# Attention and two expert layers in one program: another rate for recording attention, and another start for the second head pair

## The chip, the cores and the metric

The kernel runs on one core of a Trainium2 chip. The metric is the device time of one execution in microseconds (us), the median of several. A core has TensorE (PE, matrix products; its weight loads are PEld in the profile), VectorE (DVE), ScalarE (ACT), GpSimd (POOL) and SyncE (SP, which here issues DMAs). Each runs its own instructions in their order and waits on semaphores for the others.

## What is computed

Attention over 4 batches and 12 heads, 448 tokens of 64 features, with normalized queries and keys; then two expert layers over all 1792 tokens, the first with an ELU, the second gated, with a norm before it.

```python
def rmsnorm(x, g):
    rms = np.sqrt(np.mean(x * x, axis=-1, keepdims=True) + 1e-06)
    return x / rms * g
q_n, k_n = (rmsnorm(q, g_q), rmsnorm(k, g_k))
scores = np.matmul(q_n, k_n.transpose(0, 1, 3, 2)) / np.sqrt(64)
attn = softmax(scores)
x = np.matmul(attn, v)              # heads side by side: 1792 x 768

h = x @ w_in                        # 768 -> 2048
x = np.where(h > 0, h, np.exp(np.minimum(h, 0)) - 1) @ w_out

xn = rmsnorm(x, rms_g)
g = xn @ w_gate                     # 768 -> 1536
x = (g / (1 + np.exp(-g)) * (xn @ w_val)) @ w_out2
```

## The kernel before

**Tiles and stages.** Attention goes by head pairs: six pairs to a batch (NPB), 24 in all, numbered 0 to 23. All products of the experts split both operands into a rounded high part and the rest and run three matmuls of 128 x 448 each (`mm3`). The experts run in five stages (STAGES): first experts of batch 0, first experts of batch 1, second experts of both, first experts of batches 2 and 3, second experts of both. A first-expert stage has 16 units of six products with `xs` (the split x) and 24 units of four with `gbig` (the split activations). x of batch b is complete when its six pairs are; tile `xf` is a pair's result.

**A pair.** `load_tk` loads token rows, `squares` sums their squares (ACT, then DVE at line 555), `factors` makes the reciprocal roots `rr` of one or more pairs with 13 small DVE instructions (`rsqrt`), and `spread` spreads the factors of a pair's keys over the partitions: for pairs under FIRST by eight small matmuls against `ident` into a PSUM bank, for the others by a write to DRAM (`scr`) and two loads back (`rb`). `prep_q` and `prep_k` split queries and keys; `prep_k` multiplies by the spread factors (line 355, `rw` or, for odd pairs of batch 0, a part of `wr`). Then four groups of scores (`s_group`): matmuls, maxima (line 636, tile `nm`), a multiplication of the maxima by `rr` (line 638), exponentials (ACT, tile `p` or `pj`; for odd pairs of batch 0 a part of `tbig`). The tail of a pair is eight rounds of transposes (line 308) and copies into `pt` and `pe` and three to four products with the values. A pair counts 15 pieces: 4 groups of scores, 8 transposes, 3 products.

**Weights.** A weight chunk of 128 x 768 arrives as 64-bit floats (`wr<-wst`) and is converted once by four instructions into `wc` (two on ACT or POOL, two on DVE: lines 506 and 355), then split: a copy `w<-wc` (ACT or POOL) and a subtraction `w<-wc,w` (POOL or DVE, line 338 or 340). The 32 chunks of the first experts are kept in DRAM for the later stages.

**What sets the order.** The program is first recorded as a list of operations; `Plan.schedule` then gives each an engine and a place. It goes by estimated costs, engine by engine; of the operations that are ready it takes the one recorded first, and an operation that may run on several engines goes where it is estimated to end first. So the place in the recording is a priority. Recording: `phase(0)` records the six pairs of batch 0 (90 pieces); then each stage records its units one by one and between them pieces of the next pairs, at an even rate that reaches GOALS[s] pairs by the end of the stage: 12, 19, 24, 24, 24. Stage 1 needs pairs 6 to 11, stage 3 needs all 24. `norm` (square root on ACT with its own table, reciprocal on DVE) is recorded behind a first-expert stage.

**PSUM.** In `phase(0)` four banks take scores, three transposes, one the values' products and the spread factors; from `phase(1)` on it is two, two, one, and three for the experts' products.

## Time and profile before

| | us |
|---|---|
| median of 3 runs | 1361.91 |
| lowest and highest | 1359.98, 1365.45 |
| the profiled execution | 1362.41 |
| its span, first to last instruction | 1360.6 |
| PE busy in it | 1295.2 |
| DVE, ACT, POOL busy | 683.4, 642.0, 748.2 |

The mean granted clock of TensorE is 0.983 of full speed; the slices of the page with less than the full clock all lie in the first 374 us. A matmul's busy time is modelled and overlaps its neighbours, so a busy PE is not one at its peak: what a stretch yields is better told by how many matmuls it holds. The first expert matmul starts at 113.8 us, the second stage's first at 316.8, the third's at 525.6; the last pair's result is there at 827.2 us.

### The profile page before, as it was taken

How to read it: one execution, taken by the hardware profiler on the slowest of the kernel's cores; microseconds unless marked ns; L12 is line 12 of the kernel's file. 1: busy time of each engine (PE TensorE's matmuls, PEld its weight loads, DVE VectorE, ACT ScalarE, POOL GpSimd, SP SyncE). 2: the span in 40 equal slices, each digit the busy share in tenths (PEclk: the TensorE clock that was granted, in tenths of full speed). 3: DMA queues.
4: the chain of work that ended last, by engine and by line, in shares of the span. 5: the costliest groups of instructions: out<-in, count | busy, mean ns of one | idle time of the engine just before them, and what ended most of it. 6: DMA issues, size and time to landing. Idle time of an engine off the chain costs nothing.

```text
span 1360.6 us, 17489 instructions
## 1 busy us (share of the span) xinstructions
PE 1295.2 (95%) x6438; PEld 1058.2 (78%) x6438; DVE 683.4 (50%) x997; ACT 642.0 (47%) x1251; POOL 748.2 (55%) x571
## 2 busy tenths in 40 slices
PE   4788989988899999999999999999999999999998
PEld 2345766666577777788888788999999989999998
DVE  5686899886444559953656553102221552132332
ACT  5674767576655666655553452433223532221220
POOL 1354976684564668644564466536345664354450
PEclk9798999989999999999999999999999999999999
DMA  5466777782343445654453425221111211111112
GB/s 182 154 207 216 257 242 237 244 276 82 103 124 109 135 136 167 234 168 145 154 162 121 151 98 175 79 59 47 58 59 47 59 47 58 55 51 59 47 35 81
DMA packets 63142, 174.15 MB, mean 128 GB/s; under 512 B 11200, under 2 KB 20688, under 8 KB 63056
## 3 DMA queue, kind: packets, MB, share of 16 engines
q1 hardware_dynamic: 54064, 163.58, 37.0%
q10 hardware_dynamic: 8992, 9.46, 2.4%
q8 instruction: 50, 0.82, 0.2%
q14 instruction: 36, 0.29, 0.1%
HBM read 137.83 MB, written 35.18 MB: 127 GB/s over the span
## 4 chain that ended last, share of the span: by engine, by line
PE 75%; DVE 9%; DMA 6%; issue 3%; POOL 3%; ACT 2%; SPq 1%; ACTq 0%; DVEq 0%; POOLq 0%
PE bank L295 72%; PE bank L308 3%; DMA wr<-wst 2%; DMA tk<-tok 1%; DVE wt L506 1%; DVE nm L636 1%; DVE xs L355 1%; DMA rb<-scr 1%; DVE nm L638 1%; POOL w L340 1%; DVE wc L355 1%; SPq L376 1%; DVE w L338 1%; POOL gbig L340 1%; POOL ql L340 1%
## 5 line engine op out<-in xcount | busy, mean ns | idle before, releaser
L295 PE MATMUL bank<-xs,w 128*128 128x448 f32 x2880 | 617.9, 370 | 5.7 <-DVE tbig L355 2.8
L295 PEld LDWEIGHTS bank<-xs,w 128*128 128x128 f32 x2880 | 534.3, 188 | 63.4 <-issue 8.9
L295 PE MATMUL bank<-gbig,w 128*128 128x448 f32 x2016 | 437.4, 371 | 8.6 <-POOL gbig L340 4.4
L295 PEld LDWEIGHTS bank<-gbig,w 128*128 128x128 f32 x2016 | 374.4, 189 | 51.5 <-issue 6.8
L340 POOL TENSOR_TENSOR w<-wc,w 128x768 fp32r<-128x768 f32 x156 | 297.0, 1904 | 193.7 <-ACT w L320 187.0
L320 ACT ACTIVATE w<-wc 128x768 fp32r<-128x768 f32 x95 | 80.2, 845 | 191.7 <-PE bank L295 175.1
L340 POOL TENSOR_TENSOR gbig<-tbig,gbig 128x448 fp32r<-128x448 f32 x104 | 126.6, 1218 | 60.1 <-ACT gbig L320 59.0
L636 DVE TENSOR_REDUCE nm<-bank 128x1 f32<-128x448 f32 x168 | 98.1, 616 | 60.8 <-PE bank L295 59.8
L340 POOL TENSOR_TENSOR tbig<-tbig 128x448 f32<-128x448 f32 x67 | 83.7, 1249 | 74.0 <-DVE tbig L355 65.2
L355 DVE SCALAR_TENSOR_TENSOR tbig<-tbig,bank 128x448 f32<-128x448 f32 x64 | 39.3, 616 | 148.1 <-ACT tbig L363 147.9
L324 POOL TENSOR_SCALAR w<-wc 128x768 fp32r<-128x768 f32 x73 | 63.3, 867 | 91.2 <-PE bank L295 73.1
L363 ACT ACTIVATE p<-bank,nm,rr 128x448 f32<-128x448 f32 x126 | 90.1, 720 | 41.5 <-DVE nm L638 35.9
L320 ACT ACTIVATE pt<-bank 128x384 f32<-128x384 f32 (+1 forms) x161 | 69.1, 445 | 51.3 <-PE bank L308 44.1
L308 PEld LDWEIGHTS bank<-ident,p 128*128 128x128 f32 x441 | 54.1, 145 | 48.9 <-issue 26.2
L355 DVE SCALAR_TENSOR_TENSOR wc<-wc,wt 128x768 int32<-128x768 int32 x68 | 78.4, 1152 | 26.3 <-ACT wc L488 18.4
L320 ACT ACTIVATE gbig<-tbig 128x448 fp32r<-128x448 f32 x93 | 53.7, 577 | 71.5 <-DVE tbig L338 46.0
L308 PE MATMUL bank<-ident,p 128*128 128x128 f32 x441 | 76.3, 288 | 11.6 <-ACT p L363 5.6
L363 ACT ACTIVATE tbig<-tbig 128x448 f32<-128x448 f32 x112 | 64.2, 577 | 46.9 <-DVE tbig L338 43.9
L338 DVE TENSOR_TENSOR tbig<-bank,tbig 128x448 f32<-128x448 f32 x48 | 29.7, 621 | 102.9 <-PE bank L295 102.9
L338 DVE TENSOR_TENSOR ybig<-bank,ybig 128x448 f32<-128x448 f32 x72 | 44.5, 620 | 59.0 <-PE bank L295 59.0
L295 PE MATMUL bank<-pt,rv 128*64 128x448 f32 x252 | 70.1, 589 | 3.4 <-ACT pt L320 3.4
L506 DVE TENSOR_SCALAR wt<-wr 128x768 uint16<-128x768 uint16 x68 | 66.7, 980 | 0.4
(96 smaller groups left out, 1195.5 us busy)
## 6 DMA issues: line engine op xcount, KB each, us to landing
wr<-wst SPq DMA_DIRECT2D x68, 768.0 KB
wc<-kept SPq DMA_DIRECT2D x100, 384.0 KB
kept<-wc SPq DMA_DIRECT2D x68, 384.0 KB
rw<-qk SPq DMA_DIRECT2D x21, 512.0 KB
tk<-tok SPq DMA_DIRECT2D x20, 480.0 KB
rv<-vr SPq DMA_DIRECT2D x24, 256.0 KB
out_t<-ybig SPq DMA_DIRECT2D x24, 224.0 KB
rb<-scr ACTq DMA_DIRECT2D x36, 128.0 KB
```

Source lines behind the costliest of these rows:

```text
L295: T.matmul(o, l, r, start=start, stop=stop)
L308: T.transpose(o, i, ident)
L320: alts["a"] = (c_a(n), lambda: A.activation(out=dst, in_=src, func=AF.Copy))
L324: lambda: G.tensor_scalar(out=dst, in0=src, scalar1=1.0, scalar2=0.0, op0=ALU.mult, op1=ALU.add),
L338: alts["v"] = (c_tt(a, b, n), lambda: V.tensor_tensor(out=dst, in0=a, in1=b, op=op))
L340: alts["g"] = (0.25 + 0.0022 * n, lambda: G.tensor_tensor(out=dst, in0=a, in1=b, op=op))
L355: {"v": (c_tt(a, b, size(dst)), lambda: V.scalar_tensor_tensor(out=dst, in0=a, scalar=s, in1=b, op0=op0, op1=op1))},
L363: {"a": (c_a(size(src)) + extra, lambda: A.activation(out=dst, in_=src, func=func, **kw))},
L376: {by: (cost, lambda: q.dma_start(out=dst, in_=src))},
L506: vop(0.15 + 0.00104 * WN, lambda: V.tensor_scalar(out=th, in0=h16, scalar1=0x8000, scalar2=None, op0=ALU.bitwise_and), [th], [h16])
L636: vop(c_v1(S), lambda nm=nm, ot=o[t]: V.tensor_reduce(out=nm, in_=ot, axis=AX.X, op=ALU.max, negate=True), [nm], [o[t]])
L638: vop(0.4, lambda: V.tensor_tensor(out=nm, in0=nm, in1=d["rr"][:, both], op=ALU.mult), [nm], [nm, d["rr"][:, both]])
```

## The change

Three edits. FIRST is 2, so the factors of pair 1 too are spread by matmuls (and the host lays out that pair's token rows to fit). The start of `attention` is written in another order: the loads of pair 1's queries and keys come earlier, the factors of pair 1 are made alone and those of pairs 2 and 3 and of pairs 4 and 5 in two chains, in place of one chain for all five; `prep_q` and `prep_k` of pair 1 come ahead of the squares of the later pairs. GOALS is 13.25, 19.75, 24, 24, 24, so 7.25 pairs are recorded in the first expert stage in place of 6, 6.5 in the second in place of 7, and 4.25 in the third in place of 5.

```diff
-FIRST = 1
+FIRST = 2
...
         load_consts()
-        for i in range(1, 4):
-            load_tk(i)
+        load_tk(1)
+        load_rw(1)
+        load_tk(2)
+        load_tk(3)
         squares(0)
         factors(0, 0, 1)
         spread(0)
-        load_rw(1)
         prep_q(0)
         prep_k(0)
-        for i in range(1, NPB):
-            squares(i)
-            if i + 3 < NPB:
-                load_tk(i + 3)
-        factors(0, 1, NPB)
+        squares(1)
+        load_tk(4)
+        factors(0, 1, 2)
         spread(1)
         load_v(0)
+        prep_q(1)
+        prep_k(1)
+        squares(2)
+        squares(3)
+        load_tk(5)
+        factors(0, 2, 4)
         load_rw(2)
+        squares(4)
+        squares(5)
+        factors(0, 4, 6)
         dma(rg, rmsg, 4096)
         ts(ones, ident, 0.0, 1.0, ALU.mult, ALU.add)
-        prep_q(1)
-        prep_k(1)
         load_v(1)
         spread(2)
...
-    GOALS = [12, 19, 24, 24, 24]
+    GOALS = [13.25, 19.75, 24, 24, 24]
...
-        goal = PIECES * GOALS[s]
+        goal = int(PIECES * GOALS[s])
```

The planner makes another order of it on every engine. Three places follow.

On DVE at the start, in before, from pair 0's key product (`rw`) to the second of its maxima (`nm`); `ss`, `rr` and `sn` are the sums, factors and scratch of the row factors:

```order
L355 SCALAR_TENSOR_TENSOR rw<-rw,gsc,bank_136 128x512
L555 TENSOR_REDUCE ss_115<-tk 128x15
L636 TENSOR_REDUCE nm_121<-bank_129 128x1
L555 TENSOR_REDUCE ss_115<-wr 128x15
L638 TENSOR_TENSOR nm_121<-nm_121,rr_116 128x1
L349 TENSOR_SCALAR ss_115<-ss_115 128x75
L636 TENSOR_REDUCE nm_121<-bank_130 128x1
```

The first multiplication of maxima is the fourth instruction behind the key product. The same engine in after, the last rows before that multiplication:

```order
L636 TENSOR_REDUCE nm_121<-bank_129 128x1
L355 SCALAR_TENSOR_TENSOR rr_116<-sn_118,rr_116 128x30
L355 SCALAR_TENSOR_TENSOR wr<-wr,gsc,bank_136 128x512
L338 TENSOR_TENSOR sn_118<-rr_116 128x30
L555 TENSOR_REDUCE ss_115<-wr 128x15
L338 TENSOR_TENSOR sn_118<-sn_118,ss_115 128x30
L349 TENSOR_SCALAR ss_115<-ss_115 128x30
L355 SCALAR_TENSOR_TENSOR rr_116<-sn_118,rr_116 128x30
L349 TENSOR_SCALAR rr_116<-ss_115 128x30
L338 TENSOR_TENSOR sn_118<-rr_116 128x30
L349 TENSOR_SCALAR rr_116<-rr_116 128x30
L338 TENSOR_TENSOR sn_118<-sn_118,ss_115 128x30
```

Pair 1's key product (`wr`) stands right behind pair 0's first maximum; the multiplication is the 30th instruction behind pair 0's key product, and 24 of the 29 between belong to the chains of row factors.

On PE where the second expert stage begins, in before: the last rows of the stage's first three units (`xs` by `w`, five pairs of six), then the tail of pair 11 (`ident,p` are transposes, `qh`, `ql` the scores of pair 12):

```order
L295 MATMUL bank_135<-xs_88,w_102 128x448
L295 MATMUL bank_135<-xs_89,w_102 128x448
L295 MATMUL bank_135<-xs_88,w_102 128x448
L308 MATMUL bank_131<-ident,p 128x128 x3
L295 MATMUL bank_129<-qh 128x448
L295 MATMUL bank_129<-qh,ql 128x448
L295 MATMUL bank_129<-ql,qh 128x448
L308 MATMUL bank_131<-ident,p 128x128 x3
L308 MATMUL bank_132<-ident,rs_124 7x128
L308 MATMUL bank_131<-ident,p 128x128 x3
```

From there to the arrival of pair 11's x no matmul of the experts follows. In after the tail begins inside the second unit:

```order
L308 MATMUL bank_131<-ident,p 128x128 x3
L295 MATMUL bank_129<-qh 128x448
L295 MATMUL bank_129<-qh,ql 128x448
L295 MATMUL bank_129<-ql,qh 128x448
L295 MATMUL bank_134<-xs_82,w_101 128x448
L295 MATMUL bank_134<-xs_83,w_101 128x448
L295 MATMUL bank_134<-xs_82,w_101 128x448
L308 MATMUL bank_132<-ident,rs_124 7x128
L295 MATMUL bank_134<-xs_84,w_101 128x448
L295 MATMUL bank_134<-xs_85,w_101 128x448
L295 MATMUL bank_134<-xs_84,w_101 128x448
L308 MATMUL bank_131<-ident,p 128x128 x3
```

From the first of these transposes to the first matmul with pair 11's x, 27 matmuls of the experts now stand between the rows of attention.

On ACT in the same place, in before: the norm's square root (`tbig` from `eps`) with its two table loads, then the last exponentials of pair 11 (`p` with `sm`) and the first copy of its tail:

```order
L363 ACT_TABLE_LOAD
L363 ACTIVATE tbig<-bank_135,eps 128x448
L320 ACTIVATE qh<-rw 128x512
L363 ACT_TABLE_LOAD
L363 ACTIVATE p,sm_120<-bank_129,nm_122,rr_117 128x448
L363 ACTIVATE p,sm_120<-bank_130,nm_122,rr_117 128x448
L320 ACTIVATE pt<-bank_131 128x384
```

In after, from the last of these exponentials to the table load:

```order
L363 ACTIVATE p,sm_120<-bank_130,nm_122,rr_117 128x448
L363 ACTIVATE tbig<-ybig 128x448
L320 ACTIVATE pt<-bank_131 128x384
L320 ACTIVATE rt_125<-bank_132 7x128
L376 DMA rsum_188<-rt_125 6x128
L320 ACTIVATE gbig<-tbig 128x448
L320 ACTIVATE pt<-bank_131 128x384
L320 ACTIVATE pe<-bank_132 64x384 x2
L376 DMA rsum_188<-rt_125 2x1x64
L320 ACTIVATE pt<-bank_131 128x384
L363 ACTIVATE pj,sm_119<-bank_129,nm_121,rr_116 128x448
L320 ACTIVATE pt<-bank_132 128x384
```

The load and the square root follow behind the last row shown; they stood ahead of the exponentials and now stand inside the tail. On DVE the reciprocal of the norm likewise stood ahead of the last multiplication of pair 11's maxima (line 638) and now stands 23 rows behind it. Up to the first row that writes `xs` from `ybig` for batch 0, DVE holds 80 maxima in place of 78, and 2 weight subtractions in place of 6; ACT holds 11 weight copies in place of 15 and 13 first conversions (`wc`) in place of 18.

## Rows read from the trace of the kernel before

**Rows 1.** the page: busy time of each engine, then PE in 40 slices of the span

```profile
PE 1295.2 (95%) x6438; PEld 1058.2 (78%) x6438; DVE 683.4 (50%) x997; ACT 642.0 (47%) x1251; POOL 748.2 (55%) x571
...
PE   4788989988899999999999999999999999999998
```

**Rows 2.** stretches: length, busy time (instructions) by engine, granted clock, DMA

```profile
0.00:113.80 113.80, 80.67 (x381) 42.63 (x381) 77.86 (x156) 74.13 (x171) 46.16 (x47) 0.91 0.56 183
113.80:316.80 203.00, 186.38 (x913) 138.24 (x912) 168.82 (x226) 133.76 (x264) 147.87 (x109) 0.97 0.74 240
316.80:357.25 40.45, 32.24 (x144) 19.32 (x143) 20.56 (x40) 22.36 (x54) 14.59 (x12) 0.87 0.18 58
357.25:505.00 147.75, 147.75 (x798) 112.80 (x799) 71.67 (x121) 88.45 (x206) 90.04 (x71) 1.00 0.41 130
505.00:580.00 75.00, 72.10 (x369) 55.28 (x368) 70.56 (x83) 48.31 (x94) 57.10 (x43) 1.00 0.60 202
...
853.90:1360.60 506.70, 502.44 (x2453) 460.09 (x2452) 136.39 (x182) 147.91 (x238) 243.56 (x179) 1.00 0.18 55
```

**Rows 3.** timeline of DVE, ACT, SP at the start: start, length, instruction, idle before

```profile
15.15 0.75 DVE L355 SCALAR_TENSOR_TENSOR rw<-rw,gsc,bank 128x512 f32<-128x512 f32 x1 [1.01 <-PE bank L295]
...
35.84 0.75 DVE L355 SCALAR_TENSOR_TENSOR wr<-wr,gsc 128x512 f32<-128x512 f32 x1 [2.71 <-DMA rb<-scr]
...
20.54 0.72 ACT L363 ACTIVATE pj<-bank,nm,rr 128x448 f32<-128x448 f32 x1 [2.19 <-DVE nm L638]
...
29.73 2.23 SPq L376 DMA_DIRECT2D scr<-rr  x5
32.05 1.15 SPq L376 DMA_DIRECT2D wr<-scr  x2
```

**Rows 4.** the same as rows 2, of the first two pairs

```profile
17.50:69.00 51.50, 38.55 (x160) 20.06 (x160) 32.80 (x72) 32.62 (x78) 14.58 (x15) 0.87 0.44 139
```

**Rows 5.** groups by shape on DVE: count, busy us, mean ns, idle before

```profile
L636 DVE TENSOR_REDUCE nm<-bank 128x1 f32<-128x448 f32 x168 | 98.1, 616 | 60.8 <-PE bank L295 59.8
...
L338 DVE TENSOR_TENSOR w<-wc,w 128x768 fp32r<-128x768 f32 x12 | 17.4, 1450 | 5.5 <-POOL w L324 4.9 <-ACT w L320 0.6
...
L338 DVE TENSOR_TENSOR sn<-rr 128x15 f32<-128x15 f32 x3 | 0.5, 175 | 0.1
```

**Rows 6.** groups by shape on POOL

```profile
L340 POOL TENSOR_TENSOR w<-wc,w 128x768 fp32r<-128x768 f32 x156 | 297.0, 1904 | 193.7 <-ACT w L320 187.0 <-DMA rb<-scr 1.9
...
L324 POOL TENSOR_SCALAR w<-wc 128x768 fp32r<-128x768 f32 x73 | 63.3, 867 | 91.2 <-PE bank L295 73.1 <-issue 7.6 <-DVE wc L355 4.3
...
L491 POOL TENSOR_SCALAR wc<-wr 128x768 f32<-128x768 f32 x29 | 29.5, 1018 | 22.8 <-DMA wr<-wst 17.7 <-DVE tbig L355 2.2 <-DVE w L338 1.5
```

**Rows 7.** instructions on tile nm: count, ns min/median/max, first and last start

```profile
L638 DVE TENSOR_TENSOR nm<-nm,rr x96: 99/351/1811, 20.4 to 789.4; 128x2 f32<-128x2 f32 x72, 128x1 f32<-128x1 f32 x24
```

**Rows 8.** timeline of PE where the second expert stage begins

```profile
326.79 3.92 PE L295 MATMUL bank<-xs,w 128*128 128x448 f32 x18
...
350.66 0.47 PE L295 MATMUL bank<-xs,w 128*128 128x448 f32 x1
...
357.25 3.91 PE L295 MATMUL bank<-xs,w 128*128 128x448 f32 x18 [2.69 <-DVE tbig L355]
```

**Rows 9.** timeline of ACT, then DVE, in the same place

```profile
324.87 1.28 ACT L363 ACT_TABLE_LOAD   x1
...
330.97 0.72 ACT L363 ACTIVATE p<-bank,nm,rr 128x448 f32<-128x448 f32 x1 [2.29 <-DVE nm L638]
...
327.97 2.94 DVE L371 RECIPROCAL tbig<-tbig 128x448 f32<-128x448 f32 x1
```

**Rows 10.** stretches in the same place, columns as in rows 2

```profile
330.50:350.70 20.20, 15.42 (x60) 6.88 (x57) 6.87 (x24) 8.16 (x20) 0.01 (x1) 0.75 0.19 55
...
336.00:346.00 10.00, 8.53 (x26) 3.99 (x26) 2.97 (x11) 4.33 (x11) 0.00 (x0) 0.52 0.16 46
346.00:351.00 5.00, 5.00 (x25) 1.95 (x22) 1.46 (x3) 2.02 (x6) 0.31 (x1) 1.00 0.14 23
```

## The prediction, made before the run

> **What bounds the kernel now.** I read the page first, then one table of busy times by stretch, then the timelines at the two places where TensorE has gaps. The page gives TensorE 95% of the span, and its 40 slices show where the rest is: the first slices and a shallow hollow up to the eleventh [rows 1]. The table of stretches makes that exact [rows 2]. From 853.9 us on there is no attention left and 2453 matmuls take 506.7 us, 0.2066 us each: TensorE is the bound, and no reordering changes that. Where attention and experts are mixed and TensorE has no gap (357.25 to 505 us) one record costs 147.75/798 = 0.185 us. I use that as the price of mixed work and ask of each earlier stretch what it took beyond it:
>
> - 0 to 113.8 us (first batch's attention): 381 records are worth 70.5 us; 43 us are lost.
> - 113.8 to 316.8 us (first expert stage): 913 are worth 169 us; 34 us are lost. DVE is busy 168.8 of 203 us, POOL 147.9.
> - 316.8 to 357.25 us (the second expert stage begins while the last pair of batch 1 is still open): 144 are worth 26.6 us; 13.8 us are lost, at a granted clock of 0.87.
> - 505 to 580 us (end of the second stage, begin of the third): 369 are worth 68.3 us; 6.7 us are lost, with DVE busy 70.6 of 75.
>
> The number of matmuls is the same in both kernels but for the spread of one pair's row factors (eight small ones), so the change can only move these four losses, about 97 us together. Everything behind 580 us is bounded by TensorE and simply starts earlier or later.
>
> **The change part by part.**
>
> *Term A, the start.* Removed: the second pair's way of its key factors through DRAM, one small write and two loads on SP's queue (0.43 us of the 2.23 us for five writes, and 1.15 us) with their landing time. In before, the key product of pair 1 starts at 35.84 us, having waited 2.71 us for that load, while that of pair 0, fed from PSUM, starts at 15.15 [rows 3]. In after it stands right behind the first maximum of pair 0, so at about 20 us. Added: two more chains of 13 small DVE instructions, 26 in all; the 15-wide ones take 0.175 us [rows 5], and at 0.2 us for all it is 5.2 us. The order shows where they stand: between pair 0's key product and the first multiplication of its maxima there are 24 of them and pair 1's key product, where there were none. So pair 0's first exponential, at 20.54 us in before [rows 3], comes later by 24 x 0.2 + 0.75 = 5.5 us. Who waits behind it: ACT's exponentials of pair 0, then TensorE's transposes. What goes the other way: in the stretch of the first two pairs DVE idles 51.5 - 32.8 = 18.7 us [rows 4], and pair 1, ready 14 us sooner, can fill that. Bounds: +5.5 us if pair 0's delay passes through all six pairs; -4 us if half of the idle time is filled (9.4) less the 5.2 us added. Neither is nearer, since DVE is busy 78 of 113.8 us and ACT 74 [rows 2]: I take 0.
>
> *Term B, the first expert stage.* The rate of 7.25 pairs is one of recording only; what runs is what the planner orders. Up to the first row of the second norm's input, DVE's order holds 80 maxima in after against 78 in before. The stage thus takes in two maxima more, not the 1.25 pairs of nine: its TensorE work grows little, and what it takes in is missing later, where TensorE is the bound. What moves is the load among the engines. DVE gives four of six weight subtractions to POOL, 4 x 1.450 = 5.8 us less on DVE [rows 5]; POOL gets these at 1.904, four weight copies at 0.867 and five conversions at 1.018 from ACT: 7.6 + 3.5 + 5.1 = 16.2 us more [rows 6]. Bounds: -6 us, as DVE is the busiest engine of the stage; +8 us if half of what POOL gets falls where POOL is the late one. POOL would stand at 164 of 203 us, level with DVE at 163. I take +1 us.
>
> The Trainium skill (SBUF — State Buffer, Who interferes with whom) speaks against this part: a DVE instruction with two SBUF inputs contends with a GpSimd instruction that reads SBUF, and the loser waits for the whole of it. The trace agrees as far as it goes: the multiplication of maxima, two tiny SBUF inputs, takes 99 ns at the least and 1811 ns at the most, about one POOL subtraction [rows 7, 6]. By the rule alone DVE would lose most of the 5.8 us again, and the sum would be some 5 us higher.
>
> *Term C, the begin of the second expert stage.* In before, TensorE runs its first three products up to the last pair's share, the last run of them starting at 326.79 us; then there is only the tail of pair 11 until its x arrives, and the next product starts at 350.66, the fourth unit at 357.25 us [rows 8]. Ahead of the tail ACT loads a table at 324.87 (square root of the norm), DVE takes 2.94 us for its reciprocal at 327.97, and only then come the last exponentials, at 330.97 us [rows 9]. From 330.5 to 350.7 us TensorE does 60 short records in 20.2 us, and from 336 to 346 at a clock of 0.52, the lower of its two levels for most of it, after the gaps of the tail began; 26 records take 10 us there, and 25 take 5 us right behind, at full clock [rows 10]. In after's order the last scores stand before the new stage's first product, the last exponentials ahead of the table load and the reciprocal, and the transposes of the tail start inside the second unit: 27 expert matmuls lie between the rows of attention until pair 11's x arrives. These are 27 x 0.2066 = 5.6 us of work that ran ahead of the tail and now runs in its gaps; with them the fall of the clock should go, 10 - 26 x 5/25 = 4.8 us. Bounds: -13.8 us, the whole loss, and -3 us if the tail's chain through ACT keeps its length and only its start moves. Value: -10 us.
>
> *Term D, the end of the second stage.* Goal 19.75 in place of 19 leaves 4.25 pairs, not 5, for the third stage; 0.75 x 7 x 0.616 = 3.2 us of maxima [rows 5] leave the stretch around it, where DVE is nearly full. Bounds -6.7 (the whole loss) and 0; value -2 us, since most of that DVE time lies after 580 us, where it costs nothing.
>
> The remaining edits (the loads' order on SP, the second pair's token layout) move transfers by about one issue each, 0.43 us, ahead of work that ACT and DVE reach later: nothing.
>
> Sum: 0 + 1 - 10 - 2 = -11 us. The profiled execution took 1362.41 us (span 1360.6), 0.5 above the median of 1361.91; so 1351.4 for it, and 1351 us by the median.
>
> **The rivals.** About 0.5%, 6.8 us, is what a measurement of this kernel can tell from no change.
>
> *The tail keeps its length.* Pair 11's tail is a chain of transposes and copies between TensorE and ACT over two banks, and nine DMA issues stand among ACT's copies in after too. Then the fillers do not shorten it: C is -3, D 0, B +1: 1360 us. For it: ACT is busy only 8.2 of 20.2 us there [rows 10], so latency rules. Against it: the late exponentials, which the new order mends.
>
> *POOL becomes the bound of the first stage* (the slower side). Its added 16.2 us come whole if its idle time there, 55 us [rows 2], is all waiting for ACT's weight copies, as most of its idle time before a subtraction is (187 us over the run [rows 6]), and so can't be filled. Price: +16 in B, +2 in A, -10 in C, so +8: 1370 us. It decides once more than 14 us of the added POOL time end up on the path. By the skill's rule of the shared port it would be likelier than by POOL's busy share.
>
> *The start pays in full.* Pair 1's early keys fill DVE's idle time: A -4, B -4, C -10, D -2: -20, so 1342 us.
>
> **How the numbers follow.** My forecast (1346 to 1357 us) has 0.47, the tail that keeps its length 0.23, POOL as the bound 0.12, the paying start 0.18. The predicted time is the forecast's, 1351 us. The range 1338 to 1366 us holds the first, the second and the fourth with their bounds and leaves out POOL's case and the ends. Faster by over 0.5% means under 1355.1 us: most of the forecast (0.42) and the fourth case, 0.60. Within 0.5%: 0.28, the second case and the rest of the forecast. Slower: 0.12.
>
> **What would show it.** C is right if after shows expert matmuls between the transposes of the last pair of batch 1, the clock at full level there, and some 10 us less from the end of the first stage to the fourth unit of the second. A: pair 1's key product near 20 us, pair 0's first exponential near 26, and the first expert matmul still within 5 us of 113.8. B: POOL busy near 164 us in a stage as long as before. D: fewer than 6.7 us lost between the stages. I am wrong if the first stage ends more than 8 us late, or if the first expert matmul moves by over 6 us either way: then the start, which I priced at nothing, decides.

## The result, and the profile after

The changed kernel takes 1345.84 us (median of 4 runs, 1342.86 to 1346.72) where the kernel before took 1360.95 beside it (1357.18 to 1365.45): a ratio of 0.9884 [0.9849, 0.9918]. In a second set of runs it was 0.9928 [0.9900, 0.9956]. Both say faster; what both intervals hold is 0.8 to 1.0%. The profiled execution of after took 1346.72 us, its span is 1344.9, so 15.7 us less than the span of before.

The page of after: busy time of each engine, then the tenths of 40 slices [rows 1].

```profile
span 1344.9 us, 17561 instructions
...
PE 1283.6 (95%) x6454; PEld 1055.7 (78%) x6454; DVE 692.1 (51%) x1010; ACT 641.1 (48%) x1253; POOL 765.4 (57%) x582
...
PE   4888989998999999999999999999999999999998
...
PEclk9889999999999999999999999999999999999999
```

The table of stretches of after, taken between the same events as [rows 2] but for the border of the fourth and fifth row, which is the begin of the third stage. Columns: stretch, its length, busy time and count of PE, PEld, DVE, ACT and POOL, granted clock, DMA share, GB/s.

```profile
0.00:107.15 107.15, 76.96 (x408) 42.68 (x409) 86.35 (x189) 72.70 (x174) 50.00 (x50) 0.94 0.60 197
107.15:308.90 201.75, 184.26 (x928) 136.98 (x927) 168.87 (x215) 132.32 (x267) 165.09 (x124) 0.98 0.74 240
308.90:336.00 27.10, 23.32 (x120) 15.90 (x118) 19.81 (x36) 19.90 (x44) 12.28 (x11) 0.98 0.27 81
336.00:518.80 182.80, 180.72 (x958) 133.84 (x959) 96.77 (x151) 110.24 (x257) 119.54 (x92) 0.98 0.46 141
518.80:838.30 319.50, 315.87 (x1595) 266.14 (x1595) 183.41 (x241) 157.99 (x276) 174.66 (x130) 1.00 0.47 153
838.30:1344.90 506.60, 502.45 (x2453) 460.15 (x2452) 136.85 (x182) 147.99 (x238) 243.79 (x179) 1.00 0.18 55
```

What is to be seen: the first expert matmul came at 107.15 us (before 113.8), so 6.7 us earlier (in a second profile of after it is 109.6, 4.2 us earlier). Of the 27 more PE records done by then, 16 are the spread of pair 1's factors, which only after does on TensorE (eight matmuls, each of them two records). The first expert stage is as long as it was, 201.75 against 203.0. The begin of the second stage shrank from 40.5 to 27.1 us. From its fourth unit on (336.0 in after, 357.25 in before) to the end it is 1008.9 us where it was 1003.3: 5.6 of the 21 us that were won by then are given back. The last stretch, 506.6 us, did not change at all.

At the start, the key product and the first exponential of after [rows 3]; columns: start, duration, engine, line, operation, tiles, and the idle time before it with what ended it.

```profile
15.71 0.75 DVE L355 SCALAR_TENSOR_TENSOR rw<-rw,gsc,bank 128x512 f32<-128x512 f32 x1 [0.43 <-PE bank L295]
...
22.64 0.75 DVE L355 SCALAR_TENSOR_TENSOR wr<-wr,gsc,bank 128x512 f32<-128x512 f32 x1 [1.40 <-PE bank L295]
...
26.54 0.72 ACT L363 ACTIVATE pj<-bank,nm,rr 128x448 f32<-128x448 f32 x1 [1.56 <-DVE nm L638]
```

Pair 1's keys are multiplied at 22.64 us, 13.2 us earlier, and pair 0's first exponential is at 26.54, 6.0 us later, where about 20 and about 26 were said.

At the begin of the second expert stage (TensorE, ACT and the clock; [rows 8 to 10]):

```profile
308.87 3.81 PE L295 MATMUL bank<-xs,w 128*128 128x448 f32 x18
312.51 0.49 PE L308 MATMUL bank<-ident,p 128*128 128x128 f32 x3
...
336.02 3.73 PE L295 MATMUL bank<-xs,w 128*128 128x448 f32 x9 [3.53 <-DVE tbig L355]
```

```profile
312.00 0.19 ACT L363 ACTIVATION_READ_ACCUMULATOR p<-bank,nm,rr 128x1 f32 x1
...
319.00 1.28 ACT L363 ACT_TABLE_LOAD   x1
...
325.06 1.28 ACT L363 ACT_TABLE_LOAD   x1
```

```profile
335.00:342.00 7.00, 5.98 (x18) 5.29 (x19) 4.05 (x8) 3.05 (x7) 5.67 (x6) 0.52 0.73 243
```

The transposes of pair 11's tail begin inside the second unit (18 matmuls in, of 15 to a unit without pair 11's share), the last exponentials of pair 11 (312.0) stand ahead of the norm's table load (319.0), and there is one wait left, 3.53 us, ahead of the fourth unit. The clock still falls there to the lower of its two levels (1.2 of 2.4 GHz; 0.52 granted), behind the begin of that wait, for 7 us in place of 10; over the whole stretch it is 0.98 in place of 0.87.

So the size of the forecast (1351 us, range 1338 to 1366) was right. Whether its reasons were is another question: the change consists of a new start and of new goals, and the profile alone does not tell which of the two moved the fourth unit to 336 us.

### The profile page after: what moved, and what is told of

It reads as the page before. It is cut to its first block, busy times and chain, and to the rows that moved or that the text cites. A ratio compares the mean times of both kernels' runs of the same rounds, so it can differ in the third digit from the quotient of the medians.

```text
span 1344.9 us, 17561 instructions
## 1 busy us (share of the span) xinstructions
PE 1283.6 (95%) x6454; PEld 1055.7 (78%) x6454; DVE 692.1 (51%) x1010; ACT 641.1 (48%) x1253; POOL 765.4 (57%) x582
## 4 chain that ended last, share of the span: by engine, by line
PE 75%; DVE 9%; POOL 4%; DMA 3%; issue 2%; ACT 1%; ACTq 0%; DVEq 0%; POOLq 0%; SPq 0%
PE bank L295 71%; PE bank L308 3%; DVE wc L355 2%; DMA wr<-wst 1%; DVE nm L636 1%; DVE xs L355 1%; POOL w L340 1%; DVE wt L506 1%; POOL w L324 1%; DVE nm L638 1%; POOL wt L501 1%; DVE gbig L338 1%; POOL gbig L340 1%; DVE ybig L338 1%; DMA kept<-wc 0%
## 5 line engine op out<-in xcount | busy, mean ns | idle before, releaser
L295 PE MATMUL bank<-gbig,w 128*128 128x448 f32 x2016 | 435.7, 370 | 10.5 <-DVE tbig L355 5.6
L340 POOL TENSOR_TENSOR w<-wc,w 128x768 fp32r<-128x768 f32 x163 | 306.4, 1880 | 198.3 <-ACT w L320 190.7
L320 ACT ACTIVATE w<-wc 128x768 fp32r<-128x768 f32 x86 | 72.6, 845 | 174.5 <-PE bank L295 172.6
L340 POOL TENSOR_TENSOR tbig<-tbig 128x448 f32<-128x448 f32 x68 | 86.9, 1279 | 70.7 <-DVE tbig L355 66.3
L324 POOL TENSOR_SCALAR w<-wc 128x768 fp32r<-128x768 f32 x82 | 74.7, 911 | 89.4 <-PE bank L295 80.1
L355 DVE SCALAR_TENSOR_TENSOR wc<-wc,wt 128x768 int32<-128x768 int32 x68 | 82.4, 1212 | 28.0 <-ACT wc L488 23.2
L355 DVE SCALAR_TENSOR_TENSOR ybig<-bank,ybig 128x448 f32<-128x448 f32 x48 | 29.8, 623 | 78.1 <-PE bank L295 78.1
L355 DVE SCALAR_TENSOR_TENSOR tbig<-tbig 128x448 f32<-128x448 f32 x48 | 54.6, 1139 | 25.5 <-ACT tbig L363 25.2
```

The lines of the kernel that those rows point to most:

```text
L295: T.matmul(o, l, r, start=start, stop=stop)
L320: alts["a"] = (c_a(n), lambda: A.activation(out=dst, in_=src, func=AF.Copy))
L324: lambda: G.tensor_scalar(out=dst, in0=src, scalar1=1.0, scalar2=0.0, op0=ALU.mult, op1=ALU.add),
L340: alts["g"] = (0.25 + 0.0022 * n, lambda: G.tensor_tensor(out=dst, in0=a, in1=b, op=op))
L355: {"v": (c_tt(a, b, size(dst)), lambda: V.scalar_tensor_tensor(out=dst, in0=a, scalar=s, in1=b, op0=op0, op1=op1))},
```

## The experiments

Times are medians; the kernel before ran beside each set (1357.53, 1355.76, 1357.43 and 1354.08 us). All ratios are to it.

| run | us | ratio [95%] |
|---|---|---|
| goals alone | 1361.69 | 1.0016 [0.9990, 1.0042] |
| start alone | 1348.16 | 0.9931 [0.9907, 0.9954] |
| before, norm later | 1355.12 | 0.9987 [0.9961, 1.0013] |
| after, one chain | 1359.41 | 1.0022 [0.9995, 1.0049] |
| after again | 1348.71 | 0.9928 [0.9900, 0.9956] |
| after, second goal 19 | 1345.60 | 0.9918 [0.9896, 0.9939] |
| after, one chain, norm later | 1359.44 | 1.0029 [1.0008, 1.0050] |
| after, second pair by DRAM | 1363.24 | 1.0040 [1.0019, 1.0062] |
| before, pair 6 alone | 1343.97 | 0.9895 [0.9869, 0.9921] |
| second pair by DRAM, pair 6 alone | 1342.97 | 0.9896 [0.9874, 0.9919] |
| after, pair 6 alone | 1341.98 | 0.9900 [0.9873, 0.9928] |
| the same, second goal 19 | 1343.67 | 0.9896 [0.9859, 0.9934] |

### First set: which half of the change is it

**Goals alone**, on the kernel before:

```diff
-    GOALS = [12, 19, 24, 24, 24]
+    GOALS = [13.25, 19.75, 24, 24, 24]
-        goal = PIECES * GOALS[s]
+        goal = int(PIECES * GOALS[s])
```

> The kernel before with the new recording goals alone (13.25 and 19.75 pairs in place of 12 and 19); the start is the old one. Theory of places: the gain of after is a sum of two places, the start (first expert matmul 113.8 to 107.2 us) and the begin of the second expert stage (316.8 to 357.3 us, 40.5 us long, in after 27.1). Then here the first expert matmul stays at 113.8 us, the begin of the second stage is some 27 to 31 us long, a third of that gain is given back in the next unit, and the time is 1352 us (ratio 0.993). Rival, the start decides alone: the time stays within 3 us of 1361. Rival, the order falls by luck: the stretch is of any length and the time lies anywhere from 1350 to 1370 with no relation to these two places.

Measured: 1.0016, no gain. The first expert matmul stayed at 113.9 us as expected, and the begin of the second stage did shrink, from 40.5 to 34.9 us (27 to 31 said); but from the fourth unit to the end it is 1008.7 us, 5.4 more than in before. The sum of places was wrong here: what the goals win at the begin of the second stage they give back behind it.

**Start alone**, on the kernel after:

```diff
-    GOALS = [13.25, 19.75, 24, 24, 24]
+    GOALS = [12, 19, 24, 24, 24]
```

> After with the old goals (12 and 19 pairs), so that the new start of the second pair is all that is changed against before. Theory of places: the first expert matmul comes at 107.2 us as in after, the begin of the second stage keeps some 40 us, the time is 1353 us (ratio 0.994). In the order of this kernel, however, pair 11's last exponentials already stand ahead of the table load of the norm and expert products stand between the tail's transposes, as in after; if that order is what shortens the tail, this stretch too shrinks by 8 to 13 us and the time is near 1346 us, so that the goals add nothing. Rival, the early start is only an early start and its gain is lost in the first expert stage, where DVE is the late engine: first expert matmul at 107 but the second stage's first product at 316 again, 1360 us.

Measured: 0.9931, some 9 us. The first expert matmul is at 108.2 us, the stretch at the begin of the second stage fell to 32.1 us, though no goal was touched. So the start carries the gain, and it carries it into a place 300 us later. The second branch of the expectation (8 to 13 us less there, near 1346 us) has the size about right; its reason, the order at the tail, is what the next run tests.

**Before, norm later**, to test what the prediction named as the cause of the long tail: the norm's table load and reciprocal ahead of pair 11's last exponentials.

```diff
-        if kind == 1 and s + 1 < len(STAGES) and STAGES[s + 1][0] == 1:
-            norm(bs[0])
```

> The kernel before, with the norm of batch 0 recorded at the begin of the second experts and not behind the first expert stage; start and goals as before. This takes the table load (324.87), the 2.94 us reciprocal (327.97) and the products with ones away from ahead of pair 11's last exponentials. Theory, the late exponentials make the hole at the tail of pair 11: the fourth unit of the second stage moves from 357.3 to some 349 us, and the time falls by 3 to 8 us (1353 to 1358), if the norm costs nothing at its new place. Rival, the tail's own chain of transposes and copies makes it, with nothing behind it that could run: the stretch stays at 40 us and the time at 1361 us. Rival, the norm stalls TensorE at its new place, where all of the second experts wait for it: 2 to 6 us slower there, 1361 to 1367 us.

Measured: 0.9987 [0.9961, 1.0013]: not to be told from before (1355.12 us lies in the theory's range, but before itself took 1357.53 beside it). The stretch fell from 40.5 to 35.4 us; of these 5 us the ratio shows 1.8, and its interval holds none of them and all. Late exponentials are a part of the hole at the most.

**After, one chain**: the factors of pairs 2 to 5 in one chain of small DVE instructions.

```diff
         squares(3)
         load_tk(5)
-        factors(0, 2, 4)
         load_rw(2)
         squares(4)
         squares(5)
-        factors(0, 4, 6)
+        factors(0, 2, 6)
```

> After with the factors of pairs 2 to 5 in one chain of 13 DVE instructions, as in before, in place of two chains. Theory: a chain costs little (26 small instructions took some 3 us in after, since they issue about 0.1 us apart), and its split matters little: first expert matmul within 2 us of 107.2, time within 3 us of 1346. Rival, the split is what lets pairs 2 and 3 go on before the squares of pairs 4 and 5 are summed: first expert matmul at 109 to 112 us, 1349 to 1352 us. Rival, each chain is paid on the path: 1 to 3 us faster.

Measured: 1.0022, the whole gain is gone, with 13 small DVE instructions less and the first expert matmul at 110.4 us, 3 us earlier than in before. No expectation came near it. The begin of the second stage is 45.4 us long here. It ends like this (TensorE of this kernel):

```profile
342.99 1.88 PE L295 MATMUL bank<-xs,w 128*128 128x448 f32 x8 [0.74 <-POOL xs L340]
...
351.71 1.49 PE L295 MATMUL bank<-xs,w 128*128 128x448 f32 x3 [6.03 <-DVE tbig L355]
```

From 341.8 us on the three open units of the second stage get the share of pair 11, all three at once (eight of its nine matmuls in the row at 342.99), and then the fourth unit waits 6.03 us until the evictions of the three have freed a bank. That led to two theories for the next set: the order at the tail (as before), or this pile, which comes whenever the units have to wait for pair 11.

### Second set: the tail, or what comes before it

**After again** and **after, second goal 19** (all else as in after, so its order is the same up to the second stage):

```diff
-    GOALS = [13.25, 19.75, 24, 24, 24]
+    GOALS = [13.25, 19, 24, 24, 24]
```

> After itself once more, beside the others of this set, so that differences of a few us among them can be read. Expected 0.988 to 0.990 of the kernel before.

> After with the second goal back at 19 pairs (13.25 stays). Its order is that of after up to the second expert stage; from there on 0.75 pair of attention moves to the third stage. The prediction gave the new goal a gain of 2 us: then this is 2 us slower than after. Rival, from the traces of the runs before: with the goal at 19.75 the time from the fourth unit of the second stage to the begin of the third is 182.8 us (after) and 182.0 (goals alone) against 169.9 (start alone) and 168.2 (before), so 13 us more for 63 records, and the third stage is 319.6 and 320.9 against 328.4 and 328.3, only 7 to 9 us less: the new goal costs 4 to 6 us, and this is 4 to 6 us faster than after (ratio to after 0.996, some 1337 to 1341 us).

Measured: 0.9928 [0.9900, 0.9956], above the 0.988 to 0.990 expected, and 0.9918 [0.9896, 0.9939]. The intervals overlap for the most part; the difference is 1.4 us by the ratios and 3.1 by the medians, on the rival's side but smaller than it said, and not to be told from nothing. The traces show why: with the goal at 19 the stretch from the fourth unit to the third stage is 172.0 us in place of 181.7, and the third stage 329.1 in place of 320.5. It is moved work. The place that the goal was to relieve, the 75 us around the begin of the third stage (505 to 580 us in before, [rows 2]), is this in after:

```profile
496.00:571.00 75.00, 71.90 (x366) 55.67 (x367) 64.08 (x76) 47.88 (x89) 56.05 (x41) 1.00 0.56 183
```

DVE is busy 64.1 us there in place of 70.6, and TensorE does 366 records in place of 369.

**After, one chain, norm later**: both edits of the first set, on after.

> After with the factors of pairs 2 to 5 in one chain, and with the norm of batch 0 recorded at the begin of the second experts. With one chain alone the begin of the second expert stage took 45.4 us, and the table load of the norm came at 314.8 us, ahead of nearly all exponentials of pair 11, its last at 330 us. Theory, that order makes the stretch long: without the norm there, it is 30 to 36 us long and the time falls by 8 to 14 us (to 1346 to 1351; ratio to before 0.990 to 0.995). Rival, the pile of evictions of the first three units, which all end with pair 11's x, makes it (6.03 us of waiting ahead of the fourth unit): then the stretch stays over 40 us and the time near 1358.

Measured: 1.0029, the stretch 43.9 us. The theory of the late exponentials fell: with the norm out of the way the stretch is as long as with it, and the fourth unit still waits 6 us.

**After, second pair by DRAM**: all of after, but the second pair's key factors take the way through DRAM as in before.

```diff
-FIRST = 2
+FIRST = 1
```

> After with the second pair's key factors by DRAM again, as in before, all else as in after (its own chain of factors, the new order, the two chains for the other four, the new goals). The start: if the spread by TensorE brought the gain, the first expert matmul is at 112 to 116 us, as in before; if the early chain and the new order brought it, it stays at 107 to 109, and pair 1's key product comes some 5 us later than the 22.6 us of after. The begin of the second stage: in this kernel's order 59 of the rows of exponentials stand ahead of the norm's table load (64 in after, 59 with one chain, whose stretch is 45.4 us), so by the theory of the late exponentials it is 41 to 46 us long, and the time 1356 to 1362 us; by the rival, that only the start decides, the time is 1346 to 1352.

Measured: 1.0040, slower than before by 0.2 to 0.6%, and the stretch is 51.8 us (41 to 46 said). The first expert matmul is at 109.0 us, nearly as early as in after. So the early first expert matmul is not what pays either.

What separates good and bad runs is seen when their events stand side by side (starts in us, read from each trace; "hole" is the time between the last maximum of pair 5 and the first of pair 6, start to start, in which no scores of attention reach DVE; "lag" is the time from the second stage's first product to pair 11's x):

```
                          first     first max    hole   2nd stage  pair 11's  lag   fourth   fourth unit
                          expert mm  of pair 6           begins     x               unit     to the end
before                    113.8      135.5       30.9    316.8      349.4      32.6  357.3   1003.3
goals alone               113.9      136.6       31.3    319.8      343.4      23.6  354.6   1008.7
norm later                116.5      137.9       30.0    316.6      344.1      27.5  352.0   1000.9 *
one chain                 110.4      141.9       45.7    306.3      340.5      34.2  351.7   1003.1 *
one chain, norm later     109.8      140.3       45.1    309.3      342.0      32.7  353.2   1003.5 *
second pair by DRAM       109.0      135.5       36.1    305.0      345.6      40.6  356.8   1008.3
start alone               108.2      125.0       29.3    314.4      338.7      24.2  346.5   1004.9
after                     107.2      123.3       27.2    308.9      327.0      18.1  336.0   1008.9
after again               109.6      126.8       28.3    312.3      330.4      18.1  339.4   1008.0
second goal 19            108.9      128.5       32.5    314.4      332.5      18.1  341.5   1002.6 *
before, pair 6 alone      116.8      109.9        8.5    317.9      336.1      18.2  344.0    999.9 *
by DRAM, pair 6 alone     114.8      111.6        6.8    321.4      329.4       8.1  340.5   1002.3 *
after, pair 6 alone       108.3      102.0        5.1    316.4      326.7      10.2  337.9   1001.8 *
same, second goal 19      105.9      100.4        5.1    318.6      328.9      10.2  340.1   1003.2 *
* the last stage took 501.6 us in this execution, 506 in the others (see the end)
```

The fourth unit comes 8 to 11 us behind pair 11's x in all of them, and from there to the end it is 1000 to 1009 us. So pair 11's x sets the fourth unit to within 3.4 us, and with it most of the time. It doesn't set all of it: one chain and start alone have their x 1.8 us apart (340.5 and 338.7), yet with the last stage set equal their profiled executions are 8.5 us apart, since one chain has 11.2 us from x to the fourth unit (7.9 with the start alone) and 3.2 us more behind it. Pair 11's x is early where pair 6 begins early, as far as the two groups go: all runs of the upper six rows have pair 6's first maximum at 135 us or later and a ratio of 0.9987 or more; the next four have it at 123 to 129 and 0.9884 to 0.9931. Within a group the order doesn't hold (one chain has the latest pair 6 and the earliest x of its six), so this is a hint, and the third set is the test. An early first stage without early attention (by DRAM: second stage at 305.0) only makes the lag longer.

Why does pair 6 begin so late? In before, this is what DVE does between pair 5 and pair 6, and then what SP's queue (SPq: the load of pair 11's tokens), ACT and its DMA queue (ACTq) do (the rows between them, of weights and other things, are left out):

```profile
104.07 1.16 DVE L636 TENSOR_REDUCE nm<-bank 128x1 f32<-128x448 f32 x2 [2.86 <-PE bank L295]
...
108.46 1.14 DVE L555 TENSOR_REDUCE ss<-tk 128x15 f32<-128x960 f32 x1
...
109.94 0.20 DVE L349 TENSOR_SCALAR ss<-ss 128x90 f32<-128x90 f32 x1
...
119.34 0.96 DVE L355 SCALAR_TENSOR_TENSOR rr<-sn,rr 128x90 f32<-128x90 f32 x1
...
131.70 0.75 DVE L355 SCALAR_TENSOR_TENSOR rw<-rw,gsc,rb 128x512 f32<-128x512 f32 x1 [8.02 <-DMA rb<-scr]
...
135.55 0.62 DVE L636 TENSOR_REDUCE nm<-bank 128x1 f32<-128x448 f32 x1
```

```profile
70.70 0.34 SPq L376 DMA_DIRECT2D tk<-tok  x1
...
102.57 0.99 ACT L363 ACTIVATE tk<-tk 128x960 f32<-128x960 f32 x1
...
120.33 3.21 ACTq L376 DMA_DIRECT2D scr<-rr  x6
...
123.88 3.75 ACTq L376 DMA_DIRECT2D rb<-scr  x2
```

The factors of pairs 6 to 11 are one chain on 128 x 90 numbers. It can't start before pair 11's squares are summed (108.46; these six pairs share one token buffer, so their squares come one after the other, the last on ACT at 102.57; its tokens had been asked for at 70.70). The chain ends at 120.30, the factors of all six pairs are written to DRAM, two loads bring pair 6's back, and DVE stands idle for 8.02 us until they land. Only then are pair 6's keys multiplied. The rows of after at the same place, those of SP's queue and ACT first, then DVE's:

```profile
70.87 0.33 SPq L376 DMA_DIRECT2D tk<-tok  x1
...
77.76 1.02 ACT L363 ACTIVATE tk<-tk 128x960 f32<-128x960 f32 x1
```

```profile
80.10 1.13 DVE L555 TENSOR_REDUCE ss<-tk 128x15 f32<-128x960 f32 x1
...
93.50 0.20 DVE L349 TENSOR_SCALAR ss<-ss 128x90 f32<-128x90 f32 x1
...
106.54 1.21 DVE L355 SCALAR_TENSOR_TENSOR rr<-sn,rr 128x90 f32<-128x90 f32 x1
...
118.55 0.75 DVE L355 SCALAR_TENSOR_TENSOR rw<-rw,gsc,rb 128x512 f32<-128x512 f32 x1
...
123.25 0.62 DVE L636 TENSOR_REDUCE nm<-bank 128x1 f32<-128x448 f32 x1 [0.46 <-PE bank L295]
```

The tokens of pair 11 are asked for at the same time as in before (70.87 and 70.70 us); what moved is the place of its square in ACT's order, 77.76 in place of 102.57. The squares are summed at 80.10 us, 28 us earlier. Of these, 13.2 us are left at the key product: the chain starts only 12.3 us behind the sum, so here it is not the squares that it waits for, and it takes 14.3 us (93.5 to 107.75) in place of 10.4. With one chain it is as late as in before (DVE of that kernel):

```profile
109.72 1.16 DVE L555 TENSOR_REDUCE ss<-tk 128x15 f32<-128x960 f32 x1 [0.23 <-ACT tk L363]
...
126.86 0.26 DVE L355 SCALAR_TENSOR_TENSOR rr<-sn,rr 128x90 f32<-128x90 f32 x1
...
135.13 0.75 DVE L355 SCALAR_TENSOR_TENSOR rw<-rw,gsc,rb 128x512 f32<-128x512 f32 x1 [2.08 <-DMA rb<-scr]
```

### Third set: the chain of the second batch by itself

If that is the cause, one edit there must do what the change did, with nothing of the change in it, and it must also mend the bad variant. The factors of pair 6 are made alone, behind its own squares:

```diff
-        for i in range(NPB, 2 * NPB):
+        load_tk(NPB)
+        squares(NPB)
+        factors(1, 0, 1)
+        load_rw(NPB)
+        spread(NPB)
+        for i in range(NPB + 1, 2 * NPB):
             load_tk(i)
             squares(i)
-        factors(1, 0, NPB)
-        load_rw(NPB)
-        spread(NPB)
+        factors(1, 1, NPB)
```

On the kernel before:

> The kernel before with one edit: the factors of pair 6, the first of the second batch, are made alone behind its own squares, and its keys' spread is recorded there, in place of one chain for pairs 6 to 11 behind the squares of all six. Start and goals as before. What the runs so far show: the time at which the fourth unit of the second stage starts is that of pair 11's x plus 8 to 11 us in all of them, and from there to the end it is 1003 to 1009 us; and pair 11's x is early where pair 6 is early. Pair 6's key product is at 118.6 us in after, 121.6 with the start alone, 129.9 to 135.1 in before and the slow variants, since the chain of the six waits for pair 11's squares (108.5 us in before, and the chain ends at 120.3). Theory, this chain is the place: pair 6's key product comes at 115 us or earlier, pair 11's x at 336 to 343 us in place of 349.4, the time is 1347 to 1353 us (ratio to before 0.991 to 0.996) although nothing of the change is in it. Rival, the recorded rate or DVE's load sets pair 11, whenever pair 6 begins: pair 11's x stays at 347 to 350 and the time at 1356 to 1360.

On the variant with the second pair by DRAM:

> The variant with the new order and goals but the second pair's factors by DRAM, which took 1363 us, with the same edit as the run before this: pair 6's factors alone. Theory of the second batch's chain: its slowness was not the way of pair 1's keys but pair 6's key product at 129.9 us; with that at 115 or earlier the begin of the second stage falls from 51.8 to 27 to 36 us and the time to 1344 to 1351 (ratio 0.991 to 0.996). Rival, the way of pair 1's keys decides: the time stays at 1359 to 1365.

On after:

> After with the same edit, pair 6's factors alone. In after the chain of six ends at 107.7 us already and the key product is at 118.6. Theory: some of those 118.6 us are still waiting, so pair 6 moves by 5 us or less and the time by 0 to 5 us (1342 to 1347; ratio to before 0.986 to 0.992). Rival, with pair 6 that early its work takes DVE and TensorE time from the end of the first batch, the first expert matmul comes later, and nothing is gained: 1348 to 1352.

Measured: 0.9895, 0.9896 and 0.9900. The kernel before with this edit alone, old start and old goals, is as fast as after. The variant by DRAM went from 1363 to 1343 us. After gains nothing that can be told over its own 0.9884 and 0.9928. There the expectation was wrong in between: pair 6 began not 5 but 21 us sooner (102.0 for 123.3), and still pair 11's x came at 326.7 us, as in after (327.0 and 330.4), while the first stage grew from 201.7 to 208.1 us. A reading that fits, and that no run tests: with the hole that short, attention and experts only trade time with each other. On before with the edit, DVE does this (first the key product of pair 6, then the last maxima of pair 5 and the first of pair 6), and TensorE has this left of its wait:

```profile
69.43 0.75 DVE L355 SCALAR_TENSOR_TENSOR rw<-rw,gsc,rb 128x512 f32<-128x512 f32 x1 [2.01 <-DMA rv<-vr]
...
100.89 1.14 DVE L636 TENSOR_REDUCE nm<-bank 128x1 f32<-128x448 f32 x2
...
109.89 0.61 DVE L636 TENSOR_REDUCE nm<-bank 128x1 f32<-128x448 f32 x1
```

```profile
343.98 5.42 PE L295 MATMUL bank<-xs,w 128*128 128x448 f32 x18 [0.90 <-DVE tbig L355]
```

The hole in attention is 8.5 us in place of 30.9, pair 11's x comes at 336.1 (expected 336 to 343), and the time is lower than expected. By DRAM, the begin of the second stage fell from 51.8 to 19.1 us, more than expected, to a time just under the expected range (1344 to 1351). The first expert matmul is later than in before, 116.8 against 113.8 us, and the time is less all the same.

So one edit at this chain does as much as the whole change, and it mends the bad variant. How the gain gets from pair 6 to pair 11 is not as plain. With the start alone and in after, the first maxima of pairs 6 to 11 all lie 9 to 15 us ahead of those in before: the lead is handed on. On before with the edit, pair 6 leads by 25.6 us, but pair 8's first maximum is at 200.1 us as in before, and pair 11's leads by 8.2 again (293.8 for 302.0). No run follows that.

**The last run**: after, pair 6 alone, and the second goal at 19.

> After with pair 6's factors alone and with the second goal back at 19 pairs (13.25 stays): the first and second expert stages' begin as in the run with that edit on after, the fourth unit at 337 to 341 us. With the last stage's own length set equal (501.6 us), the runs took 998 to 1003 us from the fourth unit to the end with the goal at 19 and 1002 to 1005 with 19.75. Theory: 1338 to 1342 us, ratio to before 0.986 to 0.990, that is 0 to 4 us less than with 19.75. Rival, the goal's work is only moved and comes back whole in the third stage: the same time as with 19.75, ratio 0.990.

Measured: 0.9896 [0.9859, 0.9934], as with 19.75 (0.9900). That is the rival's number, but the interval holds the theory's 0.986 to 0.990 too; with the last stage equal in both profiles, the way from the fourth unit to the end is 1003.2 us and 1001.8 with 19.75, which also says rival. The four variants with pair 6 alone beat before, but can't be told from after or from one another, so no version here beats after beyond doubt.

## Why the prediction was right or wrong

Its number was right (1345.84 us, 0.2 under the forecast's 1346 to 1357, and 0.9928 in the second set, which is 1351), and in good part by luck. The sum said 0, +1, -10 and -2 us for the four places; the profiles say -6.7, -1.2 and -13.4 up to the fourth unit and +5.6 behind it: errors that in large part cancel. Its "wrong if" speaks against its reasons too: in the first profile of after the first expert matmul moved by over 6 us (6.7; by 4.2 in the second one), the case in which "the start, which I priced at nothing, decides". By the runs the start alone is 0.9931 and the goals alone 1.0016; the sum had 0 for the start and all of its -11 at the places that it read from the goals and the order at the tail.

- **Term A (start, 0; bounds +5.5 and -4): mis-sized.** Its single steps came true: key product of pair 1 at 22.64 us (about 20 said), pair 0's first exponential at 26.54 (about 26). Its price of the small instructions came out as well: the 24 behind pair 0's key product were charged 4.8 us and cost DVE 4.2 (22 of them start every 0.09 to 0.12 us or so, two took 0.99 and 0.97 beside a POOL instruction), and the first exponential was 6.0 us late for 5.5 said. What failed was the conclusion. The first expert matmul came earlier than the bound of -4 (by 4.2 to 6.7 us in the four profiles that have the whole new start and one chain for pairs 6 to 11), and the term was asked only for that matmul. What decided, by the third set, was another thing that the new start moved: the square of pair 11 (sum at 79.9 us with the start alone, 108.5 in before; those of pairs 6 to 9 come later than in before, that of pair 10 at the same time), and with it pair 6 by 10.5 us in the start-alone run (first maximum 135.5 to 125.0). Pair 11's x moved by 10.7 us there, and the fourth unit by 10.8.
- **Term B (first stage, +1): its size right.** Length 201.75 against 203.0 us, POOL busy 165.1 us (164 said), and POOL did not become the bound. Seen by stretch the stage is unchanged; what changed in it no busy time shows: the first maxima of pairs 6 to 11 come 11 to 14 us earlier than in before, the first expert matmul 6.7 and the second stage's first 7.9.
- **Term C (begin of second stage, -10): right in place and near in size (-13.4), wrong in cause.** The order of table load and exponentials, on which the term stood, is not it: norm later gives no gain on before, and one chain with norm later leaves 43.9 us. By the runs 8.4 us of the shrinking come with the start alone and 5.6 with the goals alone. The stretch is as long as the lag of pair 11 behind the experts plus 8 to 11 us. Of the 22.4 us by which pair 11's x comes sooner, the goals carry some (6.0 us alone, and 8 to 12 between start alone and after), but alone they don't carry it into the time; on top of the new start the two sets leave anything from nothing to some 6 us (after 0.9884 and 0.9928, start alone 0.9931).
- **Term D (end of second stage, -2; bounds -6.7 and 0): the wrong sign.** With both new goals the way from the fourth unit to the end is 3 to 6 us longer (1008.0 to 1008.9 against 1003.3 and 1004.9), which takes back what they win ahead of it. The bound stopped at 0; that more attention ahead of the third stage could cost was excluded without a row. DVE got emptier where the term wanted it, and TensorE got no further for it (the row in the second set). The run with the goal at 19 shows it as moved work: -9.7 us in the second stage, +8.6 in the third.
- **The rivals.** The tail that keeps its length, and POOL as the bound, did not come. "The start pays in full" (1342 us, 0.18) has the right owner, but most of its gain was not made in front of the first expert matmul: with the start alone that came 5.6 us earlier, and the fourth unit 10.8.

The row that would have shown it stood in the trace of before: DVE's longest idle time ahead of the second stage, 8.02 us before a key product, ended by a DMA of pair 6. The prediction reads the start until 69 us and the tail from 325 us on, and between them only sums by stretch, in which TensorE has work.

**What stays open:** why the planner puts pair 11's squares at 80 us with two chains and the spread by TensorE, and at 110 us with one chain or by DRAM. That it does is in the traces, and in before it isn't the load of the tokens (with one chain and by DRAM the load is late too, 94.9 and 104.0 us, behind pair 10's squares in the same buffer); the orders come from ready times and estimates all along the start, and no run took that apart. Delaying the squares alone, with all else as in after, wasn't tried. Nor is it followed how the lead of pair 6 reaches pair 11 in the kernels with its own chain.

## What to carry to other kernels

Where two streams of work share an engine, a loss at the place where one waits for the other is set by how late the slower stream is, and that may have been decided hundreds of us earlier: follow the late stream back to its own longest hole, also where the engine that you count is busy with the other stream. A chain that serves six consumers is ready when its last input is; give the first consumer its own. And before a sum of places is believed, each half of the change should be run alone: here one half was nearly the whole gain, as far as it can be told, and half of the other one moved some 9 us from one stage to the next.

## What the hardware showed that was not expected

**Small DVE instructions overlap.** In the two chains of after, 30 wide, instructions of 0.17 to 0.19 us start 0.10 to 0.12 us apart:

```profile
25.58 0.17 DVE L349 TENSOR_SCALAR rr<-ss 128x30 int32<-128x30 int32 x1
25.70 0.19 DVE L338 TENSOR_TENSOR sn<-rr 128x30 f32<-128x30 f32 x1
25.80 0.17 DVE L349 TENSOR_SCALAR rr<-rr 128x30 int32<-128x30 int32 x1
25.92 0.19 DVE L338 TENSOR_TENSOR sn<-sn,ss 128x30 f32<-128x30 f32 x1
```

Here two chains alternate, so that neighbours don't depend on each other. Where three in a row each need the one before (128 x 15, at 13.62, 13.83 and 14.04 us), they start 0.21 us apart.

**DVE beside POOL.** In after the chain on 128 x 90 numbers took 14.3 us. Four of its 13 instructions took 0.20 to 0.25 us, the other nine 0.60 to 1.87 (10.0 us for all 13); the rest is other work of DVE between them. The longest one, with the POOL instruction beside it:

```profile
100.84 1.87 DVE L338 TENSOR_TENSOR sn<-rr 128x90 f32<-128x90 f32 x1
```

```profile
100.80 1.81 POOL L340 TENSOR_TENSOR w<-wc,w 128x768 fp32r<-128x768 f32 x1
```

The same operation takes 0.24 us at 104.34. It ends 0.10 us behind POOL's. The Trainium skill (SBUF — State Buffer, Who interferes with whom) says that a DVE instruction with two SBUF inputs contends with a GpSimd instruction that reads SBUF, and that the other waits for the whole of it; this row agrees. So POOL's work can lengthen DVE's chains of small steps.

**TensorE at the same granted clock, 2% slower over half of the last stage.** In the last stage, which is the same products in all kernels, 160 us hold 791 or 776 records, in before within one execution:

```profile
900.00:1060.00 160.00, 160.00 (x791) 148.27 (x790) 29.61 (x48) 51.15 (x86) 76.54 (x59) 1.00 0.18 55
1140.00:1300.00 160.00, 160.00 (x776) 145.31 (x775) 40.52 (x52) 39.03 (x59) 72.48 (x51) 1.00 0.17 52
```

Six of the 14 profiles have such a stretch, in one of the last stage's two halves (before, start alone and after in the second; goals alone, second pair by DRAM and after again in the first), and a last stage of 506 us; the other eight take 501.6. It falls on any kernel, good or bad, and its 5 us can be a part of the scatter of one kernel's runs (1351 to 1366 us for before). What it is, the profile doesn't show.
